# Second product two blocks behind the first, with ten kept groups of h, in a gated linear attention plus MLP kernel

## The chip, the cores and the metric

The kernel runs on one core of one Trainium2 chip. The metric is the device time of one execution in microseconds (us); the time before is the median of three runs. The profile was taken by the hardware profiler in a further execution. PE is TensorE's matmul row and PEld its weight loads, DVE is VectorE, ACT is ScalarE, POOL is GpSimd, SP is SyncE, which here issues nearly all DMAs.

## The reference

An attention with a decaying state is followed by two products with an activation between them. All inputs are float32, except that the two weight matrices reach the kernel as 8-byte floats and are rounded on the chip.

```
# q, k, v, f_logit: (4, 8, 768, 48)
f = 1.0 / (1.0 + np.exp(-f_logit))
for t in range(S):
    state = f[:, :, t, :, None] * state + np.einsum('bhd,bhe->bhde', k[:, :, t], v[:, :, t])
    y[:, :, t] = np.einsum('bhd,bhde->bhe', q[:, :, t], state)
x = y.transpose(0, 2, 1, 3).reshape(3072, 384)
# w_in: (384, 2048), w_out: (2048, 384)
h = x @ w_in
sp = np.maximum(h, 0.0) + np.log1p(np.exp(-np.abs(h)))
g = h * erf(sp)
return g @ w_out
```

## The kernel before

The 3072 tokens are cut into 24 chunks of 128 tokens, six for each batch entry, and three chunks make a block, so there are eight blocks of 384 tokens.

**Attention of a chunk** has four stages. `stage_d` makes running sums of the logarithms of the decays by one matmul with a triangular matrix (`ps_d`), takes Exp of them in both signs on ScalarE (`dp`, `dm`), sends the last row of `dp` by four small DMAs into `Tall` (the decay total of the chunk), and multiplies q and k by them (`qd`, `kd`). `stage_t` transposes `qd` and `kd` (`ps_t`, copied to `qT`, `kT`). `stage_s` makes the scores `sc`, masks them into `A` on VectorE, makes the state's addition `dS` and updates the state `Mbd` with `Tall`. `stage_y` makes the output `y` of the chunk, which ScalarE copies into `xT`. `prepare` turns the loaded logits `lt` of a block into logarithms of decays.

**First product of a block** (`hidden`): 2048 hidden features in four groups of 512, each group 12 matmuls of 128x384 into two PSUM tiles `hps`, copied into one of seven buffers `Hg`, by ScalarE in the first two blocks and by VectorE in the others. **Activation of a group** (`activate`): ten steps on ScalarE (Exp, Ln, four Square, Tanh, with table loads between the kinds) and VectorE (four products of line 158 and the last multiplication, line 442). A group starts six steps after the one before it. **Second product** (`project`): 48 matmuls for a block, in the order group, token tile `tt` (three of 128 tokens), feature. Its sums lie in two PSUM tiles `ops`, the first of which holds token tiles 0 and 1 (line 500). After the last feature of a token tile ScalarE copies it into a spare buffer and SP sends it out. `hps` and `ops` share one PSUM pool of two buffers.

**Rounding** (`round_piece`): each weight matrix comes in eight pieces. A piece is an Abs on ScalarE (line 265) and six operations on VectorE (lines 266 to 289). Its raw words wait in some buffer that is not yet in use (`raw_home`): part of the second weight's place, an `Hg`, or a spare buffer.

**The order** is written out by hand; each engine executes its instructions in program order. After the first block's attention, iteration `it` goes through slots, one product matmul each. It strews in the attention stages of block `it+1`, rounding steps (`weights_step`), DMAs of weight pieces (`load_more`) and activation steps (`act_step`) by the number of the slot. Iteration 0 is the first product of block 0; iterations 1 to 7 hold the first product of block `it` and the second product of block `it-1`; iteration 8 is the second product of block 7. In iteration 7 the fourth group of the first product is cut into the second one (line 544).

Of the kernel before, what the change touches and what calls it, by code (L numbers as in the profile page):

```python
# [72 lines left out]
def kernel(  # L73
# [99 lines left out]
    NV, NQ, NG = 4, 3, 7  # L173
# [9 lines left out]

    spares = [fixed(f"spare{i}", [P, FG * TB], pool=fix) for i in range(3)]
# [28 lines left out]
    rounded = [0]  # L213


    def raw_home(i):
        if i < n_pieces:
            where = ["w", "w", "w", "w", 4, 5, 6, 3][i]
            at = i
        else:  # L220
            where = [4, 5, 6, "w", "w", "s0", "s1", "s2"][i - n_pieces]
            at = {3: 2, 4: 3}.get(i - n_pieces)
        if where == "w":
            m = 2 * n_ft // n_pieces
            return w_out_sb[:, bass.ts(at, m), :].rearrange("p a t -> p (a t)")
        if where in ("s0", "s1", "s2"):
            return spares[int(where[1])][:]
        return Hgs[where][:].rearrange("p a t -> p (a t)")


    AFTER = {8: 4, 9: 5, 10: 6, 11: 2, 12: 3}

    def load_piece(i):

        assert i not in AFTER or AFTER[i] < rounded[0]
# [13 lines left out]
    def round_piece(i):  # L249
# [15 lines left out]
        nc.scalar.activation(out=dst, in_=high.bitcast(FP32), func=AF.Abs)  # L265
        nc.vector.tensor_scalar(
# [49 lines left out]

    def stage_d(g):
        blk, j = divmod(g, CPB)
        if blk == 0:
            ps = ps_moe.tile([P, 2, 512], FP32, name="ps_d0", tag="moe")[:, 0, 0:d_model]  # L320
        else:
            ps = ps_at.tile([P, 512], FP32, name="ps_d", tag="at")[:, 0:d_model]
        nc.tensor.matmul(ps, lhsT=tri[:], rhs=lts[blk][:, j, :], start=True, stop=True)  # L323
        dp = dps[g % 2]
        dm = work1.tile([P, d_model], FP32, name="dm", tag="dm")
# [3 lines left out]
        nc.scalar.activation(out=dm[:], in_=ps, func=AF.Exp)  # L329
        for a in range(HP):  # L330
            nc.sync.dma_start(
                out=Tall[:, g, a : a + 1],
                in_=dp[P - 1 : P, 2 * a : 2 * a + 2, :].rearrange("o r d -> o (r d)"),
            )
# [5 lines left out]
            out=kds[g % 2][:, :, 0:D],  # L340
            in0=kns[g % NQ][:].rearrange("t (h d) -> t h d", d=D),
            in1=dm[:].rearrange("t (h d) -> t h d", d=D),
            op=ALU.mult,
        )

    def stage_t(g):
# [8 lines left out]
        kTs[g] = work1.tile([P, HP, P], FP32, name="kT", tag="kT")  # L355
        nc.scalar.copy(out=qTs[g][:], in_=pss[0][:])  # L356
# [175 lines left out]
    def slots(it):  # L532
# [4 lines left out]
        if it == n_blocks:  # L537
            return project(last)
# [388 lines left out]
```

## Time and profile before

| what | us |
|---|---|
| median of the runs | 699.82 (698.77 to 700.18, 3 runs) |
| the profiled execution, its own time | 698.7 |
| its span, first to last instruction | 697.0 |
| PE busy | 637.7 (91%) |
| DVE busy | 474.7 (68%) |
| ACT busy | 499.4 (72%) |
| POOL busy | 66.2 (9%) |

The mean granted clock of TensorE was 0.973 of full speed. The profile's slices show where it was lower and where engines were idle; each digit is the busy share of a fortieth of the span in tenths, and in the row PEclk the clock in tenths:

```
PE   3779997859999989999999999989999899999697
DVE  3779899889776675886667684675657864688410
ACT  4247888866978969688867885679666885799600
PEclk9799999989999999999999999999999999999799
```

A product matmul counts as two records in the profile, so the 384 matmuls of each product appear as x768.

### The profile page before, as it was taken

What the parts mean: (1) busy time and instruction counts of PE and PEld (TensorE: products, weight loads), DVE (VectorE), ACT (ScalarE), POOL (GpSimd) and SP (SyncE); (2) the same over time, 40 slices, a digit from 0 to 9 for tenths busy, and PEclk for the clock granted to TensorE, in tenths of its full rate; (3) what the DMA queues carried; (4) which work ended last, traced back from release to release, by engine and by line L of the source; (5) the groups of instructions that cost most, each with busy time, mean ns of one, the idle gap of its engine ahead of it and who ended that gap; (6) DMA issues with size and microseconds to landing.
All of it is one profiled execution on the core that took longest, in us unless ns stands there. A gap on an engine that the chain in (4) does not pass through costs nothing.

```text
span 697.0 us, 9216 instructions
## 1 busy us (share of the span) xinstructions
PE 637.7 (91%) x3729; PEld 389.4 (56%) x3729; DVE 474.7 (68%) x441; ACT 499.4 (72%) x456; POOL 66.2 (9%) x61
## 2 busy tenths in 40 slices
PE   3779997859999989999999989999899999999697
PEld 2546554435666555666566656666566655555353
DVE  3779899889776675886667684675657864688410
ACT  4247888866978969688867885679666885799600
POOL 0022101000112100011010110012001200000000
PEclk9799999989999999999999999999999999999799
DMA  9896740110411004110321004110200000000001
GB/s 210 197 261 189 199 113 6 29 35 1 103 34 35 1 22 82 35 35 1 84 54 35 1 11 91 35 35 0 57 13 1 0 12 24 1 0 0 24 12 37
DMA packets 122544, 36.89 MB, mean 53 GB/s; under 512 B 114304, under 2 KB 117376, under 8 KB 122496
## 3 DMA queue, kind: packets, MB, share of 16 engines
q1 hardware_dynamic: 118336, 35.45, 22.2%
q10 hardware_dynamic: 4160, 0.79, 0.7%
q8 instruction: 31, 0.51, 0.3%
q14 instruction: 17, 0.14, 0.1%
HBM read 31.46 MB, written 4.72 MB: 52 GB/s over the span
## 4 chain that ended last, share of the span: by engine, by line
PE 63%; ACT 15%; DVE 13%; issue 5%; DMA 2%; SPq 1%; POOL 0%; DVEq 0%; ACTq 0%; POOLq 0%
PE ops L509 27%; PE hps L476 24%; ACT x L153 6%; DVE e L158 6%; PE y L147 4%; PE sc L368 3%; PE ps_t L352 2%; ACT e L439 2%; PE ps_d L323 1%; DMA lt<-in_f_logit_dram 1%; ACT L439 1%; PE dS L387 1%; ACT L300 1%; ACT yl L428 1%; DVE A L373 1%
## 5 line engine op out<-in xcount | busy, mean ns | idle before, releaser
L509 PE MATMUL ops<-w_out_sb,Hg 128*128 128x384 f32 x768 | 268.6, 502 | 16.5 <-ACT spare L518 16.5
L476 PE MATMUL hps<-xT,w_in_sb 128*128 128x384 f32 x768 | 260.3, 491 | 9.8 <-ACT Hg L489 5.8
L158 DVE SCALAR_TENSOR_TENSOR e<-x,e 128x1536 f32<-128x1536 f32 x128 | 230.0, 1797 | 22.7 <-ACT x L153 18.4
L153 ACT ACTIVATE x<-yl,serf_bias 128x1536 f32<-128x1536 f32 x128 | 196.7, 1568 | 22.1 <-DVE e L158 21.8
L509 PEld LDWEIGHTS ops<-w_out_sb,Hg 128*128 128x128 f32 x768 | 146.0, 195 | 118.6 <-ACT spare L518 20.8
L476 PEld LDWEIGHTS hps<-xT,w_in_sb 128*128 128x128 f32 x768 | 143.6, 191 | 108.8 <-ACT Hg L489 7.6
L442 DVE TENSOR_TENSOR Hg<-Hg,e 128x1536 f32<-128x1536 f32 x32 | 56.2, 1757 | 51.3 <-ACT e L439 51.2
L439 ACT ACTIVATE e<-e 128x1536 f32<-128x1536 f32 x32 | 47.5, 1484 | 29.7 <-DVE e L158 29.5
L491 DVE COPY Hg<-hps 128x768 f32<-128x768 f32 x48 | 45.8, 955 | 32.6 <-PE hps L476 32.4
L339 POOL TENSOR_TENSOR kd<-kn,dm 128x384 f32<-128x384 f32 x21 | 32.2, 1535 | 375.0 <-issue 208.7
L424 ACT ACTIVATE e<-Hg 128x1536 f32<-128x1536 f32 x32 | 47.3, 1477 | 4.7 <-DVE Hg L491 4.7
L428 ACT ACTIVATE yl<-e 128x1536 f32<-128x1536 f32 x32 | 47.5, 1485 | 0.5
L518 ACT COPY spare<-ops 128x384 f32<-128x384 f32 x24 | 11.3, 471 | 45.9 <-PE ops L509 45.7
L403 POOL TENSOR_TENSOR Mbd<-Sn,Tall 48x192 f32<-48x192 f32 x32 | 32.8, 1025 | 109.7 <-DVE Sn L400 74.9
L373 DVE TENSOR_TENSOR A<-sc,tri 128x1024 f32<-128x1024 f32 x24 | 29.3, 1220 | 14.3 <-PE sc L368 14.1
L147 PE MATMUL y<-A,vt 128*32 128x128 f32 x768 | 36.9, 287 | 1.7 <-DVE A L373 0.9
L147 PEld LDWEIGHTS y<-A,vt 128*32 128x32 f32 x768 | 28.4, 112 | 15.4 <-issue 9.2
L300 ACT ACT_TABLE_LOAD x27 | 34.6, 1283 | 1.3 <-PEq L911 0.8
L335 DVE TENSOR_TENSOR qd<-qn,dp 128x384 f32<-128x384 f32 x24 | 13.3, 556 | 32.2 <-ACT dp L326 32.2
L439 ACT ACT_TABLE_LOAD x27 | 34.6, 1283 | 0.5
L368 PEld LDWEIGHTS sc<-qT,kT 48*128 48x128 f32 x384 | 23.7, 190 | 15.0 <-issue 11.5
L356 ACT COPY qT<-ps_t 128x512 f32<-128x512 f32 x24 | 13.9, 580 | 23.8 <-PE ps_t L352 23.7
(69 smaller groups left out, 391.5 us busy)
## 6 DMA issues: line engine op xcount, KB each, us to landing
lt<-in_f_logit_dram SPq DMA_DIRECT2D x24, 192.0 KB, 3.7
qn<-in_q_dram SPq DMA_DIRECT2D x24, 192.0 KB, 3.5
out_dram<-spare SPq DMA_DIRECT2D x24, 192.0 KB, 1.9
kn<-in_k_dram SPq DMA_DIRECT2D x22, 192.0 KB, 3.6
vt<-in_v_dram SPq DMA_DIRECT2D x22, 192.0 KB, 3.7
w_out_sb<-in_moe_w_in_dram SPq DMA_DIRECT2D x4, 768.0 KB, 5.8
Hg<-in_moe_w_in_dram SPq DMA_DIRECT2D x4, 768.0 KB, 8.3
Hg<-in_moe_w_out_dram SPq DMA_DIRECT2D x3, 768.0 KB, 4.7
```

What stands on the lines that cost most here:

```text
L147: nc.tensor.matmul(y[M * i : M * (i + 1), kt, :], lhsT=terms[n][0], rhs=terms[n][1], start=(n == 0), stop=(n == len(terms) - 1), skip_grou ...
L153: nc.scalar.activation(out=dst[:], in_=y[:], func=AF.Square, bias=serf_bias[:, i : i + 1], scale=SERF_K)
L158: nc.vector.scalar_tensor_tensor(out=e[:], in0=x[:], scalar=SERF_AB[i][1], in1=e[:], op0=ALU.add, op1=ALU.mult)
L300: nc.scalar.add_instruction(mybir.InstLoadActFuncSet(act_func_set_id=EXP_LN, name=nc.get_next_instruction_name(), engine=mybir.EngineType. ...
L368: nc.tensor.matmul(sc[:, r, a, :], lhsT=kT[rows(r), a, :], rhs=qT[rows(r), a, :], start=True, stop=True,)
L424: nc.scalar.activation(out=e[:], in_=h, func=AF.Exp)
L428: nc.scalar.activation(out=y[:], in_=e[:], func=AF.Ln, scale=SERF_C, bias=1.0)
L439: nc.scalar.activation(out=e[:], in_=e[:], func=AF.Tanh)
L442: nc.vector.tensor_tensor(out=h, in0=h, in1=e[:], op=ALU.mult)
L476: nc.tensor.matmul(hps[:, j, 0:TB], lhsT=w_in_sb[:, kt, ft * P : (ft + 1) * P], rhs=xTs[blk][:, kt, :], start=(kt == 0), stop=(kt == n_k - 1),
L491: nc.vector.tensor_copy(out=to, in_=hps[:, :, 0:TB])
L509: nc.tensor.matmul(of[tt], lhsT=gr["h"][:, j, tt * P : (tt + 1) * P], rhs=w_out_sb[:, ft, :], start=(ft == 0), stop=(ft == n_ft - 1),)
```

## The change

Ten `Hg` buffers are kept in place of seven, and the second product of a block stands two iterations behind its first: iterations 0 and 1 hold a first product alone, iterations 2 to 7 hold two groups of the first product of block `it`, the second product of block `it-2`, and the other two groups; iterations 8 and 9 hold the second products of blocks 6 and 7. The spare buffers go; the last pieces of the second weight wait in `Hg` 7 to 9, and the pieces are rounded in another order. The three `vt` buffers were four. In the second product token tiles 0 and 1 are copied together once both are done, and sent by one DMA. In the first block (three chunks) the decay totals come from four matmuls of 128x1 each, copied by VectorE, in place of the DMAs. The Exp that made `dm` writes `kd` itself. The Abs of a piece is issued one piece ahead. Loads and stages of the start stand in another order, and the rate of rounding and activation steps is changed.

```diff
-    NV, NQ, NG = 4, 3, 7
+    NV, NQ, NG = 3, 3, 10
-    spares = [fixed(f"spare{i}", [P, FG * TB], pool=fix) for i in range(3)]
+    osb2 = fixed("osb2", [P, 2, d_model], pool=fix)
+    osb1 = fixed("osb1", [P, d_model], pool=fix)
...
+    HOMES = [("w", 0), ("w", 1), ("w", 2), ("w", 3), 4, 5, 6, 3] + [4, 5, 6, ("w", 2), ("w", 3), 7, 8, 9]
+    ORDER = list(range(8)) + [8 + j for j in (0, 3, 1, 4, 2, 5, 6, 7)]
...
         nc.scalar.activation(out=dst, in_=high.bitcast(FP32), func=AF.Abs)
+        yield
         nc.vector.tensor_scalar(
...
-        nc.scalar.activation(out=dm[:], in_=ps, func=AF.Exp)
-        for a in range(HP):
-            nc.sync.dma_start(
+        nc.scalar.activation(out=kd, in_=ps.rearrange("t (h d) -> t h d", d=D), func=AF.Exp)
+        if blk > 0:
+            for a in range(HP):
+                nc.sync.dma_start(
...
+        if g in totals:
+            pairs = dps[g % 2][:].rearrange("t (a r) d -> t a (r d)", r=2)
+            for a in range(HP):
+                nc.tensor.matmul(
+                    totals[g][:, a : a + 1], lhsT=pairs[:, a, :], rhs=ident[:, P - 1 : P],
+                    start=True, stop=True,
+                )
+            nc.vector.tensor_copy(out=Tall[:, g, :], in_=totals.pop(g))
...
-                    if ft == n_ft - 1:
-                        assert rounded[0] == 2 * n_pieces
-                        osb = spares[0][:, bass.ts((blk * CPB + tt) % (FG * TB // d_model), d_model)]
-                        nc.scalar.copy(out=osb, in_=of[tt])
-                        r = blk * TB + tt * P
-                        nc.sync.dma_start(out=out[r : r + P, :], in_=osb)
+                    if ft == n_ft - 1 and tt == 1:
+                        nc.scalar.copy(out=osb2[:], in_=ops[0][:, :, 0:d_model])
+                        nc.sync.dma_start(
+                            out=out[r : r + 2 * P, :].rearrange("(t p) c -> p t c", p=P), in_=osb2[:]
+                        )
+                    if ft == n_ft - 1 and tt == 2:
+                        nc.scalar.copy(out=osb1[:], in_=ops[1][:, 0, 0:d_model])
+                        nc.sync.dma_start(out=out[r + 2 * P : r + TB, :], in_=osb1[:])
...
-        if it == 0:
-            return chain(*(hidden(0, gi) for gi in range(n_g)))
-        last = n_blocks - 1
-        if it == n_blocks:
-            return project(last)
-        first = [hidden(it, gi) for gi in range(n_g - 1)]
-        head = project(it - 1)
-        if it < last:
-            return chain(*first, head, hidden(it, n_g - 1))
...
+        if it >= n_blocks:
+            return project(it - 2)
+        made = [hidden(it, gi) for gi in range(n_g)]
+        return chain(*made) if it < 2 else chain(*made[:2], project(it - 2), *made[2:])
...
-        load(1, "kv", nc.scalar)
         load_f(1)
+        load(1, "qk")
+        load_f(2)
         load_piece(0)
-        load_f(2)
-        load(1, "q")
+        load(1, "v")
         load(2)
         load_piece(1)
+        load_piece(2)
...
+        def weights_step():
+            if not in_work or len(in_work) == 1 and in_work[0][2] == 5:
+                if to_round:
+                    i = to_round.popleft()
+                    in_work.append([round_piece(i), i, 1])
+                    next(in_work[-1][0], None)
+            if in_work:
+                r = in_work[0]
+                r[2] += 1
+                if next(r[0], "end") == "end":
+                    rounded.add(r[1])
+                    in_work.pop(0)
...
         stage_d(0)
-        load(3)
-        load_piece(2)
-        weights_step()
+        load(3, "qk")
+        load_piece(3)
+        stage_t(0)
         prepare(0, 2, 3)
-        stage_t(0)
         stage_d(1)
...
-        weights_step()
+        weights_steps(2)
+        stage_y(2)
+        load(5, "v")
+        load_piece(7)
+        weights_steps(1)
         prepare(1, 0, CPB)
-        weights_step()
-        stage_y(2)
-        load_piece(7)
...
-                due += 1 if it == 0 and s < 36 else 0.6
+                due += 1 if it == 0 and s < 36 else 0.8
...
                 if it == 0:
-                    step = s >= 14 and (s % 4 == 2 if s < 36 else s % 3 == 1)
-                elif it < n_blocks - 1:
+                    step = s >= 16 and s % 8 == 4
+                elif it == 1:
+                    step = s % 4 == 2
+                elif it < n_blocks:
                     step = s % 7 in (2, 5)
                 else:
-                    step = s % 3 == 2 or it == n_blocks
+                    step = s % 3 == 2
```

How this moves instructions is shown at three places: first before, then after. The first is ScalarE's list at the end of the first block's attention (the last copies of y into `xT`, and the two decay activations on `lt` of block 1). Before:

```order
L414 COPY xT<-y 128x3x128
L314 ACTIVATE lt<-lt 128x1152
L315 ACTIVATE lt<-lt 128x1152
L414 COPY xT<-y 128x3x128
L265 ACTIVATE w_in_sb<-w_out_sb 128x3x256
```

After:

```order
L421 COPY xT<-y 128x3x128
L261 ACTIVATE w_in_sb<-w_out_sb 128x3x256
L421 COPY xT<-y 128x3x128
L311 ACTIVATE lt<-lt 128x1152
L312 ACTIVATE lt<-lt 128x1152
```

The block's last copy into `xT` now stands ahead of the two activations of the next block's decays.

The second place is TensorE's list in iteration 1 (`hps` is the first product, `ops` the second). Before, its start and the first matmuls of block 0's second product:

```order
L476 MATMUL hps<-xT,w_in_sb 128x384 x37
L323 MATMUL ps_d<-lt,tri 128x384
L476 MATMUL hps<-xT,w_in_sb 128x384 x5
L368 MATMUL sc<-qT,kT 128x128 x8
L387 MATMUL dS<-vt_94,kd_104 48x48 x8
L476 MATMUL hps<-xT,w_in_sb 128x384 x5
L352 MATMUL ps_t<-ident,qd 128x128 x4
L352 MATMUL ps_t<-ident,kd_104 128x128 x4
L476 MATMUL hps<-xT,w_in_sb 128x384
L509 MATMUL ops<-w_out_sb,Hg_110 128x384 x4
```

After, from the same point on:

```order
L480 MATMUL hps<-xT,w_in_sb 128x384 x16
L323 MATMUL ps_d<-lt,tri 128x384
L480 MATMUL hps<-xT,w_in_sb 128x384 x2
L375 MATMUL sc<-qT,kT 128x128 x8
L394 MATMUL dS<-vt_92,kd_102 48x48 x8
L480 MATMUL hps<-xT,w_in_sb 128x384 x3
L350 MATMUL ps_t<-ident,qd 128x128 x4
L350 MATMUL ps_t<-ident,kd_103 128x128 x4
L480 MATMUL hps<-xT,w_in_sb 128x384 x3
```

The attention stages of block 2 begin earlier in the iteration, and no matmul of the second product follows in it; the first one now stands behind 24 matmuls of block 2's first product.

The third place is ScalarE's list around the end of one block's second product in the middle of the program. Before, the three copies (`spare<-ops`), with activation steps between them:

```order
L518 COPY spare_117<-ops 128x384
L300 ACT_TABLE_LOAD
L428 ACTIVATE yl<-e 128x1536
L518 COPY spare_117<-ops 128x384
L414 COPY xT<-y 128x3x128
L439 ACT_TABLE_LOAD
L439 ACTIVATE e<-e 128x1536
L153 ACTIVATE x<-yl,serf_bias 128x1536 x2
L518 COPY spare_117<-ops 128x384
```

After, two copies (`osb<-ops`):

```order
L516 COPY osb_119<-ops 128x768
L446 ACT_TABLE_LOAD
L446 ACTIVATE e<-e 128x1536
L153 ACTIVATE x<-yl,serf_bias 128x1536
L521 COPY osb_120<-ops 128x384
```

The first of the three copies is gone from its place, and the second has become one of both tiles.

128 lines of the change are left out of this document (49 added, 79 removed).

## The prediction

> **What bounds the kernel now.** I read four views in this order: busy time by stretch of the span, TensorE's instructions in order of time with what ended each wait, the chain that ended last, and the groups of instructions. In the first view a row is a stretch in us, its length, the busy time of PE, PEld, DVE, ACT and POOL, the granted clock of TensorE, the DMA share and GB/s.
>
> ```profile
> 0.00:38.90 38.90, 21.41 (x270) 15.34 (x270) 21.31 (x46) 15.36 (x27) 3.43 (x12) 0.87 1.00 209
> 38.90:80.50 41.60, 39.37 (x312) 24.78 (x316) 34.99 (x44) 26.42 (x36) 8.83 (x8) 1.00 0.75 201
> 80.50:152.00 71.50, 55.87 (x304) 32.98 (x296) 64.02 (x68) 58.60 (x55) 2.80 (x2) 0.96 0.30 71
> 152.00:181.90 29.90, 28.06 (x215) 17.68 (x216) 26.63 (x28) 22.23 (x21) 4.97 (x5) 0.92 0.13 29
> 263.90:345.50 81.60, 80.97 (x475) 49.50 (x474) 56.81 (x47) 70.08 (x62) 7.82 (x7) 1.00 0.19 39
> 580.00:652.80 72.80, 65.16 (x202) 37.62 (x200) 51.67 (x38) 61.90 (x46) 0.00 (x0) 0.97 0.01 3
> ```
>
> TensorE fills the middle: 80.97 of 81.60 us. It idles in three places. Before 38.90, where the first block's attention runs alone, it is busy 21.41 us. From 80.50 to 152.00 it idles 15.6 us while VectorE is busy 64.02 of 71.50: that is the rounding of the weights. And 7.6 us go at the end, beside 61.90 us of ScalarE. The waits one by one:
>
> ```profile
> 254.93 4.50 PE L509 MATMUL ops<-w_out_sb,Hg 128*128 128x384 f32 x8 [2.48 <-ACT spare L518]
> 414.77 2.85 PE L509 MATMUL ops<-w_out_sb,Hg 128*128 128x384 f32 x8 [2.92 <-ACT spare L518]
> 494.81 4.54 PE L509 MATMUL ops<-w_out_sb,Hg 128*128 128x384 f32 x8 [2.92 <-ACT spare L518]
> 652.84 34.13 PE L509 MATMUL ops<-w_out_sb,Hg 128*128 128x384 f32 x96 [6.47 <-ACT spare L518]
> 687.55 5.43 PE L509 MATMUL ops<-w_out_sb,Hg 128*128 128x384 f32 x16 [0.57 <-ACT spare L518]
> ```
>
> All five are one wait. The first two token tiles of an output block share one PSUM tile (line 500). The second may not be written until ScalarE has copied the first out (line 518), and that copy stands behind activations.
>
> One unit price is needed, that of TensorE's own work. The chain that ended last shows the same place of the program in two blocks (start, length, what):
>
> ```profile
> 263.89 10.32 PE hps L476 x32
> 422.09 10.32 PE hps L476 x32
> ```
>
> A product matmul (128x384) is two records, so one costs 2 x 10.32/32 = 0.645 us. Between the rows lie 158.20 us for two blocks: 192 matmuls are 123.8, the wait at 414.77 is 2.9, and the rest, 31.4, is six chunks of attention, 5.2 us each. A block without waits is 77.6 us. The change leaves this work as it is, so only what surrounds it can move. My sum has four terms.
>
> **Start.** TensorE's first product matmul is at 38.98. ScalarE's and VectorE's rows before it:
>
> ```profile
> 13.30 0.52 ACT L314 ACTIVATE lt<-lt 128x384 f32<-128x384 f32 x1 [1.47 <-DVE lt L310]
> 14.28 0.57 ACT L356 COPY qT<-ps_t 128x512 f32<-128x512 f32 x1
> 36.20 1.16 ACT L314 ACTIVATE lt<-lt 128x1152 f32<-128x1152 f32 x1 [4.14 <-DVE lt L310]
> 38.47 0.46 ACT L414 COPY xT<-y 128x384 f32<-128x384 f32 x1
> 22.90 0.72 DVE L396 TENSOR_TENSOR Mbd<-dS,Tall 48x192 f32<-48x192 f32 x2 [3.51 <-DMA Tall<-dp]
> ```
>
> The copy of xT at 38.47 stands behind the next block's two decay activations, 36.20 to 38.5. The new order puts the copy first, which saves 2.3. The copy of qT at 14.28 stood behind a wait for the third chunk's logits; these are now loaded ahead of the first weight piece and used behind the copy. That and the 3.51 us wait for totals that travelled by DMA free about 2.5 us of the chain between them, most of the rest being hidden by other rows. The new total matmuls (four of 128x1 for each of three chunks) and three small copies are not in this trace: the cheapest row is nothing, the dearest that of a transposing matmul set, so 0 to 3; I take 0.8, near the 0.56 us of a chunk's sixteen 48-column matmuls.
>
> ```profile
> 16.48 0.56 PE L387 MATMUL dS<-vt,kd 128*48 128x48 f32 x16
> 10.33 1.09 PE L352 MATMUL ps_t<-ident,qd 128*128 128x128 f32 x4 [2.37 <-DVE qd L335]
> ```
>
> Start: **-4**, ends 0 (a load that now lands later takes it all) and -8 (all three waits and the slow clock, 0.87, go).
>
> **Blocks 0 and 1.** Idle in the three rows from 38.90 to 181.90 is 2.2 + 15.6 + 1.8 = 19.7 us; the clock costs 55.87 x 0.04 + 28.06 x 0.08 = 4.5. So 24 us are lost. Afterwards no second product stands there, and TensorE needs, up to the third product tile of block 2, 108 matmuls (69.7) and 6.4 chunks (33.3): 103 us. VectorE must do in that time, by its new list, what these rows price (columns: count, then busy us and mean ns, then idle before):
>
> ```profile
> L266 DVE TENSOR_SCALAR w_in_sb<-w_in_sb 128x768 f32<-128x768 f32 x8 | 5.0, 629 | 6.8 <-ACT w_in_sb L265 6.7
> L266 DVE TENSOR_SCALAR w_out_sb<-w_out_sb 128x768 f32<-128x768 f32 x8 | 4.5, 558 | 8.0 <-ACT w_out_sb L265 8.0
> L270 DVE TENSOR_SCALAR w_in_sb<-w_in_sb 128x768 uint32<-128x768 uint32 x8 | 5.3, 658 | 0.1
> L275 DVE SCALAR_TENSOR_TENSOR w_in_sb<-Hg,w_in_sb 128x768 uint32<-128x768 uint32 x4 | 3.9, 964 | 0.1
> L279 DVE TENSOR_SCALAR Hg<-w_in_sb 128x768 uint32<-128x768 uint32 x4 | 2.3, 571 | 0.1
> L284 DVE SCALAR_TENSOR_TENSOR Hg<-Hg 128x768 f32<-128x768 uint32 x7 | 6.9, 984 | 0.2
> L289 DVE TENSOR_TENSOR w_in_sb<-Hg,w_in_sb 128x768 f32<-128x768 f32 x4 | 3.8, 954 | 0.1
> L158 DVE SCALAR_TENSOR_TENSOR e<-x,e 128x1536 f32<-128x1536 f32 x128 | 230.0, 1797 | 22.7 <-ACT x L153 18.4
> L442 DVE TENSOR_TENSOR Hg<-Hg,e 128x1536 f32<-128x1536 f32 x32 | 56.2, 1757 | 51.3 <-ACT e L439 51.2
> L373 DVE TENSOR_TENSOR A<-sc,tri 128x1024 f32<-128x1024 f32 x24 | 29.3, 1220 | 14.3 <-PE sc L368 14.1
> ```
>
> A piece is 0.63 + 0.66 + 0.96 + 0.57 + 0.98 + 0.95 = 4.75; fourteen pieces are left at that point, 66.5. Nine line-158 products (16.2), two of line 442 (3.5), six A (7.3) and about 14 of smaller attention operations, decays and the first eviction of block 2 make 107.5. So TensorE must idle at least 5 us, even with VectorE never idle. VectorE was busy 99.0 of 113.1 us from 38.90 to 152.00, and its 14.8 us of waits at line 266 for the Abs on ScalarE are what filled the difference; the new code issues that Abs one piece ahead, with two VectorE operations between, against waits of about 1 us, so I take them as gone. What else the two engines lose to each other I take from the row 38.90:80.50, 2.2 in 41.6, so 5.6 in 103. With 3 for the clock, 14 are lost in place of 24: **-10**. Ends: -18 (only the 5 and 1 of clock) and 0 (VectorE at the old 99.0/113.1, so 123 against 103, with the old clock). If the Abs waits stay, that is the zero end.
>
> Group 0's activation must be done before block 2's second product asks for it. By the new list 16 activation steps stand before block 2 and 7 in its first 24 slots; a group needs 10, a new one starts every 6, so groups 0 to 2 are finished when the product begins. I cost that wait at nothing. The cover grows, since each later block has 27 steps and needs 24; without it every group of a block would wait for up to a ScalarE period, 12.8 us (below).
>
> With three buffers of v in place of four, v's load of a chunk waits on SP's queue until TensorE has done y of the chunk three earlier. Behind it stand only the totals, loads and results of later chunks, and the queue has room:
>
> ```profile
> SPq L331 <- ACT dm L329: 290.3, 18, 27.0
> ```
>
> So this, the Exp written straight into kd (its readers of two chunks earlier are done by then), and the new order of the second weight's pieces, each loaded when the piece in its place is rounded, I cost at nothing; a late piece would delay VectorE's list by its landing.
>
> **The copy, blocks 2 to 6.** The three waits above are 2.5 + 2.9 + 2.9 = 8.3. Behind two of them eight records took 4.50 and 4.54 instead of 2.85, so another 3.3. What is late next is the first product tile behind it, which needs that PSUM buffer: now both halves are copied together, while four matmuls of the third tile run, 2.6 us of cover. The old copy took 0.47, so it began 2.0 to 2.5 us after TensorE had stopped; the wider one costs 0.3 more:
>
> ```profile
> L518 ACT COPY spare<-ops 128x384 f32<-128x384 f32 x24 | 11.3, 471 | 45.9 <-PE ops L509 45.7
> L489 ACT COPY Hg<-hps 128x768 f32<-128x768 f32 x16 | 12.6, 788 | 5.4 <-PE hps L476 5.4
> ```
>
> So 2.4 to 2.9 plus 0.3 less 2.6 remain, 0.5 in each of five blocks: 11.6 - 2.5, **-9**. Ends: -12 and -2 (ScalarE as late as at 652, where the copy came 6 us behind).
>
> [...]
>
> **The end.** Idle 6.47 + 0.57, and a slow clock behind the first. Two more rows show how it comes, the clock behind the wait, and the start of ScalarE's four squarings of one group in the chain:
>
> ```profile
> 652.80:660.00 7.20, 7.16 (x13) 3.96 (x14) 4.07 (x3) 1.95 (x2) 0.00 (x0) 0.59 0.11 42
> 622.37 5.87 ACT x L153 x4
> 635.20 5.87 ACT x L153 x4
> ```
>
> The clock costs 7.16 x 0.41 = 2.9; 9.9 in all. ScalarE alone needs 635.20 - 622.37 = 12.83 us a group, 2.14 us a step; the old order gave it a step each three matmuls, 1.94 us of TensorE, so over 32 steps it fell 6.4 us behind. The new block 7 gives 27 steps in 62 us (2.30 each, no lag), then 16 in the 31 us of block 6's product: 3.3 us of lag. With the copy and what is in progress that is some 4.5 against 2.6 of cover: 2 come back, and 1 for the clock. By then all groups but the last tanh are done, so block 7's product runs through. **-7**, ends -10 and -3.
>
> **Sum.** -4 - 10 - 9 - 7 = -30. The span is 697.0, so 667.0; this execution took 698.7, 1.7 more, so 668.7; the median of the runs shown, 699.8, is 1.1 above it: **670**. All near ends give -48 (652), all far ends -5 (695). The longer result transfer (two tiles in one) I cost at nothing: its buffer is next written a block later.
>
> **Rivals.** (1) Forecast, 661 to 679: 0.50. (2) The start and the early blocks give their near ends, as the missing Abs waits and the undisturbed first blocks suggest: 652 to 661, 0.17. (3) The early term comes to nothing, since VectorE still has 107 us to do against 103 and its list is strict: -20 or less, 679 to 692; 0.21. (4) The waits move whole into the evictions and the loads, no change: 0.03. (5) Slower: ScalarE becomes the bound. In the row 263.90:345.50 it is busy 70.08 with steps always at hand; the larger backlog makes each of blocks 2 to 7 such a block. It also waits for VectorE:
>
> ```profile
> ACT e L439 <- DVE e L158: 29.5, 11, 5.5
> ACT x L153 <- DVE e L158: 21.8, 16, 3.3
> ```
>
> That is 51.3 us over 32 groups, 1.6 each, 7.2 for 4.5 groups: 77.3 against TensorE's 77.6. It decides beyond 77.6, first at the copies of qT and xT. With these waits doubled a block takes 84.5, six blocks lose 41, and the time is 670 + 41 = 711. Against it: in that very row TensorE was busy 80.97 of 81.60. 0.06. Below 652 I leave 0.03.
>
> Faster or slower begins 0.2% from the median, about what a measurement of this kernel can tell: faster 0.50 + 0.17 + 0.21 + 0.03 = 0.91, same 0.03, slower 0.06. The range 653 to 690 leaves out some 0.16.
>
> **What would show it.** First product matmul near 35; VectorE without waits at the rounding's first operation and TensorE's idle between there and block 2 near 10; no wait of the second token tile, at most 1 us at the first product tile behind; one wait of about 2 us between the last two products. A ScalarE busy over 74 us in a block, with TensorE waiting for qT or xT, would make the prediction wrong.

## The result and the profile after

| what | before | after |
|---|---|---|
| median of the runs, us | 699.88 (698.77 to 700.18, 4 runs) | 665.73 (664.27 to 666.10, 4 runs) |
| profiled execution: own time; span | 698.7; 697.0 | 666.1; 664.4 |
| PE busy, us | 637.7 | 634.9 |
| DVE, ACT busy, us | 474.7, 499.4 | 476.5, 509.0 |
| mean granted clock | 0.973 | 0.991 |

The ratio is 0.9511, with a 95% interval from 0.9493 to 0.9529: the changed kernel is 34 us faster, against 30 forecast. TensorE's busy time is nearly the same, though it now holds the new matmuls of the totals (4.4 us); what went is 30 of its 59 us of idleness, and slow stretches behind some of the waits. The stretches of the span, with the same columns as in the prediction, show where:

```profile
0.00:37.80 37.80, 26.28 (x294) 20.56 (x294) 20.45 (x46) 14.23 (x25) 3.96 (x12) 1.00 1.02 231
37.80:81.50 43.70, 40.97 (x360) 25.98 (x360) 38.90 (x51) 25.05 (x35) 8.85 (x8) 1.00 0.74 191
81.50:139.50 58.00, 50.96 (x370) 31.61 (x366) 50.81 (x60) 39.03 (x42) 7.61 (x7) 0.91 0.36 85
139.50:215.80 76.30, 75.04 (x467) 46.25 (x463) 61.93 (x54) 63.79 (x56) 8.08 (x7) 1.00 0.20 40
293.40:371.00 77.60, 77.60 (x474) 48.21 (x473) 55.45 (x45) 66.50 (x58) 8.02 (x7) 1.00 0.19 39
```

The first and the fifth row say most. The start ends only a microsecond earlier than before, and TensorE is 4.9 us busier in it. In the fifth, a whole block in the middle, TensorE is busy 77.60 of 77.60 us, while ScalarE has 66.50. The chain that ended last repeats itself without a wait, the same place of the program in two blocks:

```profile
215.81 13.10 PE hps L480 x40
292.97 13.10 PE hps L480 x40
```

Between them lie 77.2 us; the prediction had 77.6 for a block without waits. TensorE's waits by releaser (us in total, times, the longest; the 5.8 of the first row is the wait for the first logits, at the very start):

```profile
PE ps_d L323 <- ACT lt L312: 10.4, 4, 5.8
PE ps_t L350 <- DVE Sn L407: 4.1, 1, 4.1
PE ps_t L350 <- DVE qd L336: 2.9, 1, 2.9
```

The copy of finished output tiles (`osb`), which led this list before with 16.5 us, isn't in it. TensorE's and ScalarE's rows around the end of one second product, and the last two products, show how it passes (start, length, what):

```profile
203.95 4.14 PE L509 MATMUL ops<-w_out_sb,Hg 128*128 128x384 f32 x12
206.42 0.78 ACT L516 COPY osb<-ops 128x768 f32<-128x768 f32 x1
207.92 0.81 PE L480 MATMUL hps<-xT,w_in_sb 128*128 128x384 f32 x2
...
596.36 62.50 PE L509 MATMUL ops<-w_out_sb,Hg 128*128 128x384 f32 x192
626.80 0.78 ACT L516 COPY osb<-ops 128x768 f32<-128x768 f32 x1
```

The joint copy ends at 207.2, and the product that needs its buffer starts at 207.92 without a wait. The last two products run through as one row of 192 records. What is left early stands in TensorE's rows with a wait, from the first product matmul on (the two of 1.0 us and 0.5 us are left out):

```profile
37.85 2.85 PE L480 MATMUL hps<-xT,w_in_sb 128*128 128x384 f32 x8 [0.61 <-ACT xT L421]
41.88 0.91 PE L323 MATMUL ps_d<-lt,tri 128*128 128x384 f32 x2 [1.18 <-ACT lt L312]
...
114.59 1.08 PE L350 MATMUL ps_t<-ident,kd 128*128 128x128 f32 x4 [4.08 <-DVE Sn L407]
126.84 1.10 PE L323 MATMUL ps_d<-lt,tri 128*128 128x384 f32 x2 [2.96 <-ACT lt L312]
```

And VectorE at the first operation of the rounding (count, busy us and mean ns, idle before):

```profile
L263 DVE TENSOR_SCALAR w_in_sb<-w_in_sb 128x768 f32<-128x768 f32 x8 | 5.8, 731 | 0.2 <-ACT w_in_sb L261 0.2
L263 DVE TENSOR_SCALAR w_out_sb<-w_out_sb 128x768 f32<-128x768 f32 x8 | 5.3, 659 | 1.5 <-ACT w_out_sb L261 1.4
```

The long waits early are one for VectorE's `Sn` and one for the next block's decays; VectorE's own waits at the rounding fell from 14.8 us to 1.7.

### The profile page after: what moved, and what is told of

Read it like the earlier page. It is cut to its first block, busy times and chain, and to the rows that moved or that the text cites. A ratio compares the mean times of both kernels' runs of the same rounds, so it can differ in the third digit from the quotient of the medians.

```text
span 664.4 us, 9237 instructions
## 1 busy us (share of the span) xinstructions
PE 634.9 (96%) x3753; PEld 392.8 (59%) x3753; DVE 476.5 (72%) x443; ACT 509.0 (77%) x456; POOL 62.6 (9%) x61
## 4 chain that ended last, share of the span: by engine, by line
PE 66%; DVE 14%; ACT 13%; issue 4%; DMA 2%; POOL 0%; SPq 0%; DVEq 0%; ACTq 0%; POOLq 0%
PE hps L480 26%; PE ops L509 26%; DVE e L158 5%; ACT x L153 4%; PE y L147 4%; PE sc L375 3%; PE ps_t L350 3%; PE ps_d L323 2%; ACT e L446 2%; ACT L297 2%; ACT yl L435 1%; DVE A L380 1%; PE dS L394 1%; DMA lt<-in_f_logit_dram 1%; DVE Sn L407 1%
## 5 line engine op out<-in xcount | busy, mean ns | idle before, releaser
L480 PE MATMUL hps<-xT,w_in_sb 128*128 128x384 f32 x768 | 263.6, 494 | 1.9 <-DVE Hg L492 1.2
L509 PE MATMUL ops<-w_out_sb,Hg 128*128 128x384 f32 x768 | 256.1, 489 | 0.1
L509 PEld LDWEIGHTS ops<-w_out_sb,Hg 128*128 128x128 f32 x768 | 143.8, 190 | 98.3 <-issue 2.0
L449 DVE TENSOR_TENSOR Hg<-Hg,e 128x1536 f32<-128x1536 f32 x32 | 58.3, 1823 | 53.5 <-ACT e L446 53.3
L340 POOL TENSOR_TENSOR kd<-kn,kd 128x384 f32<-128x384 f32 x21 | 32.2, 1533 | 339.9 <-issue 187.6
L410 POOL TENSOR_TENSOR Mbd<-Sn,Tall 48x192 f32<-48x192 f32 x32 | 29.3, 916 | 94.3 <-DVE Sn L407 88.6
L375 PEld LDWEIGHTS sc<-qT,kT 48*128 48x128 f32 x384 | 24.9, 199 | 13.2 <-issue 11.6
L323 PE MATMUL ps_d<-lt,tri 128*128 128x384 f32 x48 | 22.6, 555 | 10.5 <-ACT lt L312 10.4
```

Of the source, the lines that this page charges most:

```text
L375: nc.tensor.matmul(sc[:, r, a, :], lhsT=kT[rows(r), a, :], rhs=qT[rows(r), a, :], start=True, stop=True,)
L449: nc.vector.tensor_tensor(out=h, in0=h, in1=e[:], op=ALU.mult)
L480: nc.tensor.matmul(hps[:, j, 0:TB], lhsT=w_in_sb[:, kt, ft * P : (ft + 1) * P], rhs=xTs[blk][:, kt, :], start=(kt == 0), stop=(kt == n_k - 1),
L509: nc.tensor.matmul(ops[tt // 2][:, tt % 2, 0:d_model], lhsT=gr["h"][:, j, tt * P : (tt + 1) * P], rhs=w_out_sb[:, ft, :], start=(ft == 0), ...
```

## The experiments

Each was profiled and timed beside the kernel before on the same chip, and its ratio is to that. Spans are those of the profiled executions: 697.0 before, 664.4 after. The medians of the kernel before lay between 699.3 and 702.3 us beside these runs, so small differences between two rows are less certain than the spans look.

| kernel | span | median (lowest to highest) | ratio (95%) |
|---|---|---|---|
| after, tiles copied apart | 696.7 | 696.72 (691.41 to 699.89) | 0.993 (0.990 to 0.996) |
| before, tiles copied together | 679.1 | 680.82 (680.46 to 684.05) | 0.972 (0.966 to 0.977) |
| one block behind, first form | 671.5 | 673.36 (672.25 to 673.78) | 0.959 (0.954 to 0.965) |
| one block behind | 669.0 | 670.88 (670.62 to 671.10) | 0.958 (0.954 to 0.962) |
| after, Abs in place | 666.5 | 668.35 (665.44 to 668.50) | 0.951 (0.946 to 0.957) |
| after, totals by DMA | 667.6 | 669.07 (668.57 to 670.68) | 0.956 (0.951 to 0.960) |
| after, totals behind the scores | 659.7 | 661.17 (660.35 to 661.44) | 0.944 (0.940 to 0.948) |
| after, half the rounding | 647.9 | 650.98 (649.56 to 654.13) | 0.931 (0.926 to 0.936) |
| totals late, fewer activation steps | 658.1 | 659.87 (654.62 to 662.84) | 0.941 (0.937 to 0.945) |
| that, less on VectorE | 655.6 | 657.23 (655.42 to 657.65) | 0.938 (0.935 to 0.940) |
| totals late, idle matmuls ahead | 659.5 | 660.92 (659.63 to 661.26) | 0.944 (0.941 to 0.946) |
| after, apart, steps kept away | 691.1 | 692.38 (691.27 to 692.88) | 0.988 (0.985 to 0.992) |

**1. The copy, taken back.** In the changed kernel each token tile is copied and sent by itself again.

```diff
-                    if ft == n_ft - 1 and tt == 1:
-                        nc.scalar.copy(out=osb2[:], in_=ops[0][:, :, 0:d_model])
...
-                    if ft == n_ft - 1 and tt == 2:
-                        nc.scalar.copy(out=osb1[:], in_=ops[1][:, 0, 0:d_model])
-                        nc.sync.dma_start(out=out[r + 2 * P : r + TB, :], in_=osb1[:])
+                    if ft == n_ft - 1:
+                        osb = (osb2[:, 0, :], osb2[:, 1, :], osb1[:])[tt]
+                        nc.scalar.copy(out=osb, in_=ops[tt // 2][:, tt % 2, 0:d_model])
+                        nc.sync.dma_start(out=out[r + tt * P : r + (tt + 1) * P, :], in_=osb)
```

> The changed kernel with the copies as before: token tile 0 is copied alone, then tile 1, then tile 2, each sent by its own DMA; all else stays. Theory (the wait comes from the shared PSUM tile and a late ScalarE, and the joint copy took it away): TensorE waits again at the second token tile, 2 to 3 us in most of blocks 0 to 5 and about 3 us in block 6, with a slow clock behind some of them; the span grows from 664.4 to 672-678. Rival (the two-block distance took the wait away, since ScalarE is less late there): at most 667.

Measured: a span of 696.7, so 32.3 us are lost. TensorE's largest wait in this kernel, by releaser:

```profile
PE ops L509 <- ACT osb L517: 19.2, 8, 3.8
```

Then the stretch of one such wait, and the one behind it, in the columns of the windows:

```profile
200.60:204.40 3.80, 0.04 (x1) 0.00 (x0) 1.76 (x1) 3.80 (x5) 0.00 (x0) 0.90 0.03 0
204.40:208.40 4.00, 3.94 (x14) 2.26 (x16) 0.00 (x0) 1.48 (x2) 0.00 (x0) 0.50 0.13 49
```

And TensorE's rows there:

```profile
204.46 2.93 PE L509 MATMUL ops<-w_out_sb,Hg 128*128 128x384 f32 x4 [3.83 <-ACT osb L517]
207.32 2.08 PE L375 MATMUL sc<-qT,kT 48*128 48x128 f32 x16
209.33 5.09 PE L509 MATMUL ops<-w_out_sb,Hg 128*128 128x384 f32 x8
```

TensorE waits in all eight second products, 19.2 us; behind a long wait it runs at half speed for 4 us and more (a clock of 0.50, scores in 2.08 us that take 1.16 elsewhere, eight product records in 5.09 instead of 2.85). The waits don't make up the loss; the other 13 us are mainly that clock (TensorE is busy 648.9 us in all, against 634.9 for the same work). The expected loss was far too small on both counts. It also follows that without the joint copy the rest of the change gains little: 696.7 against 697.0 in the spans, and 0.4 to 1.0% in the ratio.

**2. The copy alone.** The kernel before, with token tiles 0 and 1 copied and sent together, and nothing else.

```diff
-                    if ft == n_ft - 1:
...
-                        nc.scalar.copy(out=osb, in_=of[tt])
+                    if ft == n_ft - 1 and tt == 1:
+                        r = blk * TB
+                        osb = spares[0][:, 0 : 2 * d_model].rearrange("p (t c) -> p t c", t=2)
+                        nc.scalar.copy(out=osb, in_=ops[0][:, :, 0:d_model])
```

> The kernel before with the joint copy alone: tiles 0 and 1 copied and sent together. Theory: the waits of 2.5 to 2.9 us in the middle go with their clock, and the 6.5 us wait near the end shrinks to about 4 and moves to the first matmul of block 7's second product; the span falls from 697.0 to 683-687. Rival (the wait only moves to the first product tile behind the copy): 693 or more.

Measured: 679.1, 17.9 us less, more than the theory had. The stretch from block 1's end to the last block, and the one wait of this kind that is left:

```profile
182.00:560.00 378.00, 377.63 (x2257) 233.85 (x2256) 266.51 (x215) 305.22 (x261) 46.17 (x34) 1.00 0.17 35
```

```profile
642.30 31.23 PE L509 MATMUL ops<-w_out_sb,Hg 128*128 128x384 f32 x96 [3.10 <-ACT spare L518]
```

In 378 us TensorE idles 0.4: in the middle the copy alone does all that the whole change does. Between the last two products 3.1 us stay; the old order still gives ScalarE its steps there at the old rate, which the prediction gave as the cause. Parts of one change can be worth different sums in different company: the joint copy takes 17.9 us off the kernel before, and 32.3 off the changed one.

**3. One block behind.** The changed kernel with its ten groups, its start, its copies and the Abs ahead, but the second product one block behind the first, in the old slots and at the old rates. In the first form a piece of the second weight is written over before its raw words have been used, so part of that weight, and the output, is not the reference's; the second form takes the pieces in an order without that.

```diff
-    ORDER = list(range(8)) + [8 + j for j in (0, 3, 1, 4, 2, 5, 6, 7)]
+    ORDER = list(range(10)) + [11, 10, 12, 13, 14, 15]
...
-        made = [hidden(it, gi) for gi in range(n_g)]
-        return chain(*made) if it < 2 else chain(*made[:2], project(it - 2), *made[2:])
+        first = [hidden(it, gi) for gi in range(n_g - 1)]
+        head = project(it - 1)
+        if it < last:
+            return chain(*first, head, hidden(it, n_g - 1))
...
-                due += 1 if it == 0 and s < 36 else 0.8
+                due += 1 if it == 0 and s < 36 else 0.6
```

> The changed kernel with the main loop of before: second product one block behind, the cut last iteration, the rates of rounding and activation steps and the order of the second weight's pieces as before; the joint copy, the start, the Abs ahead and ten groups of h stay. Theory (the distance of two blocks is what takes the early waits and ScalarE's lag at the end away): 5 to 9 us come back in blocks 0 and 1 and 4 to 6 at the end; span 672-680. Rival (the distance gives nothing by itself): at most 667.

> As the kernel one block behind (main loop of before, joint copy, start, Abs ahead and ten groups as changed), with the pieces of the second weight rounded in the order 8, 9, 11, 10, 12 to 15, so that no piece is written over before it is read. Theory (the distance gives what is left between 671 and 664): span 669-674, with waits for the copies of h and for the state in block 1, and one of about 3 us at the end. Rival (the order of the pieces made that difference): at most 667.

Measured: 671.5 and 669.0, just past and at the near edge of what the theory had. The second form's waits in block 1:

```profile
86.10 7.98 PE L483 MATMUL hps<-xT,w_in_sb 128*128 128x384 f32 x24 [1.48 <-DVE w_in_sb L286]
...
111.30 1.52 PE L483 MATMUL hps<-xT,w_in_sb 128*128 128x384 f32 x2 [3.19 <-ACT Hg L493]
```

The first product waits for its weight and for ScalarE's evictions; between the last two products there is again a wait of 3.1 us for the copy, as in experiment 2. From the kernel before by way of experiment 2 and the second form to the changed kernel, the spans are 697.0, 679.1, 669.0 and 664.4. On this path the copy takes 17.9 us, 10.1 belong to the start, the Abs, the ten groups and the totals together, and the second block of distance, with its rates, is worth 4.6 of the 32.6, at both ends of the program (5.7 counted from the first product, which came at 36.80 here). Of the 2.5 us between the two forms, 1.7 are clock: the wait between the last two products is 3.10 us in both, and behind it the 96 records of the last product took 31.23 us in the second form, and this in the first:

```profile
633.06 32.92 PE L512 MATMUL ops<-w_out_sb,Hg 128*128 128x384 f32 x96 [3.10 <-ACT osb L519]
```

**4. The Abs in its old place.**

```diff
         nc.scalar.activation(out=dst, in_=high.bitcast(FP32), func=AF.Abs)
-        yield
         nc.vector.tensor_scalar(
...
```

`weights_step` issues one piece at a time again.

> The changed kernel with the Abs of a piece issued together with the first VectorE operation, as before. Theory (VectorE's list ends last in blocks 0 and 1, so its waits for the Abs count): VectorE waits some 10 to 14 us at that operation again, and 6 to 11 of them reach the end: span 670-676. Rival (VectorE has room, or ScalarE is early enough now): at most 666.5.

Measured: 666.5, the rival's figure and only 2.1 us more, though VectorE's waits are back:

```profile
L262 DVE TENSOR_SCALAR w_in_sb<-w_in_sb 128x768 f32<-128x768 f32 x8 | 5.1, 634 | 7.0 <-ACT w_in_sb L261 6.8
L262 DVE TENSOR_SCALAR w_out_sb<-w_out_sb 128x768 f32<-128x768 f32 x8 | 4.4, 555 | 4.3 <-ACT w_out_sb L261 4.3
```

11.3 us of waits against 1.7, for 2.1 us of the span (3.0 counted from the first product, which came 0.9 earlier here). The ratios, 0.951 for both kernels, don't tell them apart. Most of what VectorE saves at this line it waits out elsewhere. From 38 to 140 us its waits for `dp` are, in the changed kernel and then here:

```profile
DVE qd L336 <- ACT dp L326: 8.6, 5, 4.8
DVE qd L335 <- ACT dp L325: 2.1, 2, 1.2
```

**5. The totals by DMA again.**

```diff
-        if blk > 0:
-            for a in range(HP):
+        for a in range(HP):
...
```

> The changed kernel with the first block's decay totals sent by DMA, as before. Theory (the 24 matmul records of 128x1, 4.4 us, stand on TensorE's chain at the start and cost as much as the DMA's wait did): first product at 35 to 38.5, span 661.5-665.5. Rival (the matmuls save what the DMA's 3.5 us wait cost): first product at 40 or later, span 667 or more.

Measured: 667.6, and the first product at 41.94 instead of 37.85, as the rival had it. The wait that the matmuls replace is larger in the new order of loads than it was before (3.51):

```profile
27.57 0.89 PE L393 MATMUL dS<-vt,kd 128*48 128x48 f32 x16 [7.42 <-DVE Mbd L402]
```

The totals by matmul are a gain of about 4 us at the first product, 3 in the span.

**6. The totals behind the scores.** The same matmuls, issued after the chunk's scores instead of after its transposes, and their copy on VectorE behind the mask.

```diff
+        if g in totals:
+            pairs = dps[g % 2][:].rearrange("t (a r) d -> t a (r d)", r=2)
...
         A = work1.tile([P, 2, HP, P], FP32, name="A", tag="A")
...
         As[g] = A
+        if g in totals:
+            nc.vector.tensor_copy(out=Tall[:, g, :], in_=totals.pop(g))
```

> The changed kernel with the matmuls of the totals moved behind the scores of their chunk, and the copy of the totals behind the mask. Theory (they delay the decay sums of the next chunk where they stand): first product 2 to 3.5 us earlier than 37.85, span 661-662.5. Rival (the chain only moves to other engines): span 664 or more.

Measured: 659.7, first product at 32.91, more than the theory had. TensorE's rows of the second chunk's scores and the third chunk's transposes, first in the changed kernel:

```profile
25.67 2.08 PE L375 MATMUL sc<-qT,kT 48*128 48x128 f32 x16
...
28.50 0.66 PE L350 MATMUL ps_t<-ident,qd 128*128 128x128 f32 x4
```

Then with the totals later:

```profile
21.78 1.16 PE L366 MATMUL sc<-qT,kT 48*128 48x128 f32 x16
...
24.35 0.66 PE L350 MATMUL ps_t<-ident,qd 128*128 128x128 f32 x4
```

From the third chunk's transposes, where both kernels run at full speed, to the first product it is 37.85 - 28.50 = 9.35 and 32.91 - 24.35 = 8.56: 0.8 us for this chunk. If each of the three chunks gives as much, they make 2.4 (an estimate). The rest of the 4.9 goes with full speed, which comes some 6 us earlier here: the same scores take 1.16 us at 21.78, and 2.08 at 25.67 in the changed kernel. Why it comes then is not settled.

**7. Half the rounding.** Of each weight piece the last three operations on VectorE are left out, so the weights are cut short instead of rounded, and the output is not the reference's.

```diff
         yield
-        nc.vector.tensor_scalar(
-            out=halves(high), in0=halves(bits), scalar1=0xFF800000, scalar2=None,
...
-        nc.vector.tensor_tensor(out=dst, in0=low.bitcast(FP32), in1=dst, op=ALU.add)
```

> The changed kernel without the last three VectorE operations of each weight piece, so the weights are cut instead of rounded; everything else stands in the same slots. Theory (VectorE's list ends last in blocks 0 and 1): TensorE's waits of 4.1 and 3.0 us there go with their clock, 6 to 10 us in all, span 654-658. Rival (ScalarE, or the order of stages, sets that stretch): 661 or more.

Measured: 647.9, more than the theory had. The stretch from 38 to 140 in the changed kernel, and then in this one:

```profile
38.00:140.00 102.00, 92.28 (x728) 57.77 (x729) 90.02 (x111) 64.40 (x78) 16.47 (x15) 0.95 0.52 129
```

```profile
38.00:140.00 102.00, 98.47 (x760) 62.35 (x762) 68.22 (x81) 73.55 (x87) 16.02 (x16) 0.98 0.56 138
```

With 22 us less on VectorE, TensorE is busy 98.5 of 102 us. The span from the first product on is 614.7 against 626.5, 11.8 less (the start, with its first pieces, gives another 4.7). So VectorE's list does set most of what is left in blocks 0 and 1.

**8. Fewer activation steps early.** The kernel of experiment 6, with four steps fewer in iteration 1 (8 in place of 12).

```diff
                 elif it == 1:
-                    step = s % 4 == 2
+                    step = s % 6 == 4
```

> The kernel with the totals behind the scores, and 8 activation steps in iteration 1 in place of 12. Theory (VectorE's list sets blocks 0 and 1): four steps, some 5 to 7 us of VectorE, move to blocks where it has room; of the waits of 4.0, 1.6 and 1.1 us there 2 to 5 us go with their clock: span 655-658 against 659.7. Rival (the steps put off come back as waits of the second product for an activation, early or at the end): 661 or more.

Measured: 658.1, though the first product came 1.75 us later; from there on it is 623.4 against 626.8 of experiment 6. The wait for `Sn` at the end of iteration 1 shrinks from 4.04 us, with a small one ahead of it:

```profile
96.52 0.63 PE L350 MATMUL ps_t<-ident,kd 128*128 128x128 f32 x4 [1.03 <-DVE Mbd L404]
111.49 1.04 PE L350 MATMUL ps_t<-ident,kd 128*128 128x128 f32 x4 [2.51 <-DVE Sn L408]
```

Not all of the gain stays. Late in the program a small matmul on the decay totals waits longer, since a product of an activation step now stands directly ahead of its operand in VectorE's list:

```profile
530.43 0.27 PE L547 MATMUL ps_f<-ident,low 128*1 128x128 f32 x1 [2.88 <-DVE low L543]
```

In experiment 6 this wait is 1.21, and the 36 product records behind it take 11.77 us in place of 13.47. So some 6 us were gained up to there and some 3 came back: the theory holds, and of the rival a part. The medians of 6 and 8 (661.2 and 659.9) lie within the spread of 8.

**9. Less on VectorE.** The kernel of 8, with block 2's `kT` copies and its first two groups' evictions on ScalarE.

```diff
-        if g < 2 * CPB:
+        if g < 3 * CPB:
...
-                        if blk < 2:
+                        if blk < 2 or blk == 2 and gi < 2:
```

> The same, and the copies of kT in block 2 and of the first two groups of h of block 2 go from VectorE to ScalarE (some 6 us). Theory: as VectorE's list is what ends last, another 1 to 3 us go: span 653-657. Rival (ScalarE, with steps always at hand, is then late for the copies): 659 or more.

Measured: 655.6, a ratio of 0.938 to before: it beats both kernels. But from the first product on it is 623.1 against 623.4 of experiment 8, so the edit itself is worth 0.3; the rest is an earlier first product (32.48 against 34.66), in a start that the edit doesn't touch.

**10. Idle matmuls ahead.** The kernel of 6, with nine matmuls without use during the first loads.

```diff
+        warm(5)
         prepare(0, 0, 1)
...
         stage_d(0)
+        warm(4)
```

> The kernel with the totals behind the scores, and nine matmuls of 128x128 without use, five ahead of the first decay sum and four behind it, where TensorE waits anyway. Theory (the start's matmuls run at half speed, scores 2.08 against 1.16 us, since TensorE has been idle, and they stand on the chain): the scores of the first chunk take about 1.2 us, and the first product comes 2 to 5 us earlier than 32.9: span 655-658. Rival (the chain of the start is that of ScalarE, VectorE and loads, or these matmuls don't lift the clock): 659-662.

Measured: 659.5 against 659.7, no gain. TensorE's first rows:

```profile
1.95 2.50 PE L624 MATMUL warm<-tri,ident 128*128 128x128 f32 x10 [1.95 <-POOL ident masks.py:199]
5.87 1.65 PE L323 MATMUL ps_d<-lt,tri 128*128 128x384 f32 x2 [1.41 <-ACT lt L312]
```

The sums behind 2.5 us of such work still take 1.65 us, where 0.81 to 0.91 is their time at full speed, and the first chunk's scores take 1.82 us, where 1.2 was expected and experiment 6 had 1.66. That idleness is what makes the start slow was the author's theory, and this run doesn't show it.

**11. Apart, with activation kept away.** The kernel of experiment 1 with no activation steps in the last twelve slots of a second product, to see whether the shared tile costs anything when ScalarE is free.

```diff
                 elif it < n_blocks:
-                    step = s % 7 in (2, 5)
+                    step = s % 3 == 1 and not 60 <= s < 72
```

> The changed kernel with tiles 0, 1 and 2 copied apart, but no activation step in the last twelve slots of the second product of blocks 0 to 5 (the steps are made closer elsewhere, 28 in a block). Theory (the wait is ScalarE's lateness, not the sharing of the tile by itself): these six waits shrink from 3.1-3.8 to 0.6-1 us and their clock stays up; with the wait of block 6 left, the span is 670-678 against 696.7. Rival (the wait is set by the sharing, whatever ScalarE does): 688 or more.

Measured: 691.1, a time of the rival's, with 12.1 us of these waits left in place of 19.2. ScalarE's rows show that it was not free:

```profile
203.05 0.48 ACT L329 ACTIVATE kd<-ps_d 128x384 f32<-128x384 f32 x1
203.42 1.57 ACT L153 ACTIVATE x<-yl,serf_bias 128x1536 f32<-128x1536 f32 x1
204.89 0.48 ACT L517 COPY osb<-ops 128x384 f32<-128x384 f32 x1
```

No gap stands before the copy: steps issued earlier were still being worked off. So the run decides neither way, and what a shared tile costs with a prompt copy stays open.

## Why the prediction was right, point by point

The span came to 664.4 where the sum gave 667.0; all four terms have the right sign, and two of them are right for reasons that held only in part. That the sum lies so near is partly luck: the start and the early blocks fell 4.3 us short, the copy and the end gave 4.0 more than forecast.

**Start, -4; measured -1.1** (38.98 to 37.85). The same start has its first product at 36.80 to 37.38 in four other kernels (experiments 1, 3 and 11), so its gain is 1.1 to 2.2 us. The mechanism held: the copy into xT stands ahead of the decay activations, and the wait for totals is gone. Mis-sized was the totals' price, 0.8, taken from a row of matmuls with 48 columns:

```profile
L358 PE MATMUL ps_d<-ident,dp 128*128 128x1 f32 x24 | 4.4, 303 | 0.0
```

They took 4.4 us, and they stand on the chain of each chunk. Experiment 5 shows that they are still better than the DMAs. In experiment 6, with them later, the first product came 4.9 us earlier; some 2.4 of that are their place, and the rest is full speed coming sooner, whose cause is open.

**Blocks 0 and 1, -10; measured -8.6.** Idle from 37.80 to 215.80 is 2.7 + 7.0 + 1.3 = 11.0, the clock costs 50.96 x 0.09 = 4.6: 15.6 of 24.2 are left, where 14 were forecast. That VectorE's work sets most of the rest is shown by experiment 7. The reason given for the gain, that the Abs waits go, fell: they did go, but experiment 4 puts them back for at most some 3 of the 8.6, so that the size came out near is partly luck. What the forecast left out is that VectorE then waits for other things, for `dp` above all, and that two blocks without a second product leave TensorE other work to do. Experiment 3 gives the distance 4.6, part of it at the end of the program. The remaining gain lies in the ten groups, their homes for raw words and the order of loads, which no run took apart.

**The copy, blocks 2 to 6, -9; measured -11.6**, close to the near end. The 0.5 us a block that was to stay did not. The sum let the joint copy begin 2.0 to 2.5 us after the second tile was done. In four of blocks 0 to 5 ScalarE stood waiting for the tile, and in the other two the copy began about 1.1 us late (206.42; the second tile was done about a third of the way through the row at 203.95, at 205.3), which with its 0.8 us is less than the cover of 2.6. Why ScalarE is less late there was not taken apart. The choice to count the clock behind waits of 2.5 us and more was right: experiment 2 alone gives 17.9, more than this term and the next (16), and the windows of experiment 1 have the clock at 0.50 behind a 3.8 us wait. What a single wait costs in clock isn't settled by its length, as the 3.10 us wait of experiment 3 shows.

**The end, -7; measured -9.9 + 1.5 = -8.4.** The wait expected between the last two products, 2 us, is not there: the joint copy began some 2 us late (626.80; by the row at 596.36 its tile was done at about 624.7), and its 0.78 us then just fit under the cover. In experiments 2 and 3, at the old rates and the old distance, 3.1 us are; which of the two took them away is open. The 1.5 that came back was costed at nothing: "the longer result transfer". The last copy and its DMA, and then the same place before:

```profile
658.93 0.48 ACT L521 COPY osb<-ops 128x384 f32<-128x384 f32 x1 [1.78 <-PE ops L509]
659.44 0.34 SPq L522 DMA_DIRECT2D out_dram<-osb  x1
```

```profile
693.05 0.48 ACT L518 COPY spare<-ops 128x384 f32<-128x384 f32 x1 [2.10 <-PE ops L509]
```

From the start of that copy to the end of the span it is 5.5 us now, and 3.95 before. Every kernel that sends two tiles by one DMA has 5.35 to 5.6 here, and the three that send each by itself have 3.95 to 4.25, so it goes with the joint copy and sending. That the last transfer waits for the larger one ahead of it is a reading, not shown.

These give -29.7 of -32.6. Two smaller waits of the copy that the prediction's rows left out are another 1.2 (16.5 in all, 15.3 counted); 1.7 are not placed.

**The rivals.** Slower by a full ScalarE did not come: 66.50 us in a block where the prediction set 74 as the mark and 77.6 as the bound. Its waits for VectorE (columns as above) shrank instead of doubling, from 21.8 at line 153:

```profile
ACT x L153 <- DVE e L158: 14.2, 8, 3.2
```

Yet a grain of this rival seems true. With two blocks in hand ScalarE nearly always has a step to do, and I read experiment 1 so: there the copy of the first tile is late in all eight products, and eight waits and their clock take back nearly all that the rest of the change gains. The forecast's weight on the joint copy was right, and too small.

## What to carry to other kernels

A buffer whose two halves are tracked as one here made the writer of the second half wait for the reader of the first (16.5 us in all before, 19.2 in experiment 1); look for it where a short wait returns once a block, and cost it with the slow clock behind it, which here was 0.4 (the prediction's three waits) to 0.7 (experiment 1) of the waits again. An engine's waits that vanish are no gain until the trace shows what its consumers wait for next: 9.6 us of VectorE's were worth 3 at most. A small operation on the chain of a start should be priced by its own kind, at the clock that holds there, and put behind the work that others wait for.

## What the runs showed of the hardware

- **Behind some short waits TensorE ran slowly, and their length alone didn't decide.** In experiment 1 waits of 3.1 to 3.8 us are followed by stretches at a clock of 0.50 to 0.61. Before, a wait of 2.48 was followed by one at 0.62, and of two of 2.92 one was (0.62 behind it; 1.00 behind the other). One of 3.10 was in the first form of experiment 3 (the 96 records in 32.92 us), and in the second form, at the same place, it was not (31.23). In experiment 9 one of 2.03 us was (six product records in 3.59 us behind it, where 2.10 is full speed); in experiment 11 one of 2.35 us was not (four records in 1.56 us).
- **Slow for long at the start, and the clock row misses it.** In the changed kernel matmuls run at about half speed until 28 us, though TensorE is busy 17.0 of the 18 us from 10 to 28. The windows give a clock of 1.00 from 10 to 28. One of these windows, and the sixteen matmuls of 25.67 (2.08 us, above) in the next chunk:

```profile
25.00:28.00 3.00, 3.00 (x40) 2.37 (x34) 1.53 (x3) 1.07 (x2) 0.00 (x0) 1.00 0.95 271
```

```profile
32.90 1.16 PE L375 MATMUL sc<-qT,kT 48*128 48x128 f32 x16
```

The duration of a repeated row tells more than the clock beside it.

- **The matmuls of one column were not cheap.** The 24 records of 128x1 took 4.4 us, and their weight loads 4.6:

```profile
L358 PEld LDWEIGHTS ps_d<-ident,dp 128*128 128x128 f32 x24 | 4.6, 287 | 0.0
```

- **The start varies.** In four kernels that differ only later, or in work without use, the first product came between 32.5 and 34.7 us (experiments 6, 8, 9 and 10), by when full speed came: the first chunk's scores took 1.16 us at 13.49 in experiment 9, and 2.08 at 13.51 in experiment 8. A gain of a microsecond should be read from a point behind the start.
